# Queries loaded in half rows and turned on VectorE, remainder rows as one chunk, and a written order for all five engines

## The chip, the cores and the metric

The kernel runs on one core of a Trainium2 chip. The metric is the device time of one launch in microseconds (us), as the median of several runs. A profile is one execution of its own, recorded instruction by instruction. Engines are named as the profile names them: PE is TensorE's matmul, DVE is VectorE, ACT is ScalarE, POOL is GpSimd, SP issues the DMAs.

## The reference

Linear attention with two softmaxes, then a two-layer block with an odd activation:

```python
batch, n_heads, seq, head_dim = (8, 8, 576, 64)      # q, k, v
n_tokens, d_model, d_ff = (4608, 512, 2048)
q_s = softmax(q, over head_dim);  k_s = softmax(k, over seq)
kv = np.einsum('bhsd,bhse->bhde', k_s, v)
x = np.einsum('bhsd,bhde->bhse', q_s, kv)            # then (batch, seq) rows x (heads, 64) columns
h = x @ w_in
g = h - np.tanh(h)
out = g @ w_out
```

All is float32. The two large products are made of float32r matmuls on split operands (a rounded part and a remainder), three of the four cross products each.

## The kernel before

**Tiling.** The 4608 rows of x are nine chunks of 512 rows (`NCH = 9`); d_ff is sixteen tiles of 128. One *step* is one pair (chunk j, tile f). In it PE runs `ph`, twelve matmuls with 512 columns that make one tile of h in PSUM (line 568), and `po`, twelve matmuls that add the tile of g of two steps earlier (`LAG = 2`) into four PSUM tiles, one per 128 rows of output (line 651). There are 144 steps. Chunk 0 is done in two pieces, its first eight tiles ahead of chunk 1 and the rest behind it.

**The activation of a step.** From the PSUM tile `ph`, ACT makes `u` (square), `t` (tanh), `vv` (a square of u) and the mask `mk`; DVE makes `g` from u and ph (line 589), multiplies vv in (line 597), subtracts t from ph (line 594) and puts that result in where the mask is set (line 602, `cp`); ACT rounds it to `gh` (line 605); POOL makes the remainder `gl` (line 608). `gh` and `gl` are what `po` reads two steps later. These tiles have two buffers each, `ph` has two PSUM banks, `vv` and `mk` one buffer.

**Attention.** For each batch, k goes through a column maximum (`km` on DVE, `pm` transposes on PE, `mx`), a broadcast of it (`d` on POOL, `pb` on PE), a subtraction, an exponential and the products `pk` with v on PE; the normalised result is the tile `kvs`. A unit of q is 256 rows of all eight heads. Its softmax is a maximum per row and head (line 408, DVE), a subtraction (line 413, POOL), an exponential (ACT), a sum (line 421, DVE) and a product (line 447, POOL). Then every 128 rows are turned by four PE transposes into PSUM (`pt`, line 461), copied out by ACT (`qs`, line 473), and multiplied with `kvs` on PE (`px`, line 487); ACT and DVE split the result into `xh` and `xl`. Two batches have 1152 rows, nine tiles of 128, so that the last 64 rows of two batches make one tile (`rest`) and chunks and batches don't line up.

**The order.** `ORDER`, a list written by hand, sets all five engines for steps 0 to 18 with the whole weight preparation and the attention of batches 0 and 1. Behind it only PE and SP have a written order (line 784 and the loop below it), and the tool's own scheduler places the work of DVE, ACT and POOL. `prepare` (line 510) gives each attention part of a chunk a half step of the sixteen steps ahead of it.

Of the kernel before, what the change touches and what calls it, by code (L numbers as in the profile page):

```python
# [10 lines left out]
F32 = mybir.dt.float32  # L11
# [59 lines left out]
def attn_moe_kernel(  # L71
# [55 lines left out]
    kvs = [const.tile([P, NC, D], F32, name=f"kvs{i}") for i in range(3)]  # L127
# [145 lines left out]

    def kv_rows(b: int, st: dict):
# [13 lines left out]
        else:  # L288
            for n, m in enumerate((st["mh"], st["ml"])):
                d = ap.tile([P, NC, P], F32R, name=f"d{b}_{n}", tag="qs", bufs=3)  # L290
                nc.gpsimd.tensor_tensor(
                    d,
                    ident.unsqueeze(1).broadcast_to([P, NC, P]),
                    m.bitcast(F32).unsqueeze(2).broadcast_to([P, NC, P]),
                    op=ALU.mult,
                )
# [3 lines left out]
                    d.rearrange("p a m -> p (a m)"),  # L300
# [42 lines left out]
    def kv_norm(b: int, st: dict):  # L343
        nc.vector.tensor_tensor(
            kvs[b % 3],
            st["pk"][:, :, 1 : D + 1],
            st["rs"].broadcast_to([P, NC, D]),
            op=ALU.mult,
        )

    tiles = []
    for b in range(B):
        tiles += [((b, u), j) for u in range(NKP) for j in range(2)]
        if b % 2:
            tiles.append(((b, "rest"), 0))
    qs_of = {}

    def batches(i: int):
        (b, u), _ = tiles[i]
        return ((b - 1, 0, REST), (b, REST, P)) if u == "rest" else ((b, 0, P),)

    def rows_of(x: bass.AP, i: int):

        (b, u), j = tiles[i]
        if u == "rest":
            for bb, p0, p1 in batches(i):
                yield x[(bb + 1) * S - REST : (bb + 1) * S, :], p0, p1  # L370
        else:
            r0 = b * S + 2 * P * u
            yield x[r0 : r0 + 2 * P, :].rearrange("(p j) m -> p j m", j=2)[:, j, :], 0, P

    def q_load(unit):
        b, u = unit
        name = f"q{b}_{u}"
        if u == "rest":
            qt = ap.tile([P, H, 1, D], F32, name=name, tag="q", bufs=1)
            for half in range(2):  # L380
                src = q[b - 1 + half, :, S - REST :, :].rearrange("h s d -> s h d")
                nc.sync.dma_start(qt[half * REST : (half + 1) * REST, :, 0], src)
# [46 lines left out]
    def q_soft(unit):  # L429
        q_max(unit)  # L430
        q_sub(unit, nc.gpsimd)
        for part in (q_exp, q_sum, q_eps, q_inv):
            part(unit)
# [42 lines left out]
    px_of = {}  # L476

# [354 lines left out]
```

## Time and profile before

| | |
|---|---|
| time, median of 3 runs | 903.09 us (902.65 to 903.84) |
| span of the profiled execution | 901.7 us |
| PE busy | 875.9 us (97%) |
| DVE, ACT, POOL busy | 616.2, 554.2, 288.9 us |
| matmuls of L568 and L651 on the chain that ended last | 38% and 38% of the span |

The span runs from the first to the last instruction of the profiled execution; the median of the runs is 1.4 us above it. A group of matmuls is pipelined, so the time that it costs is the distance from its start to the start of the next group, not its duration. The number in square brackets behind a row of the timeline is idle time of that engine just ahead of it, with what ended it.

### The profile page before, as it was taken

The page shows a single profiled execution, that of the slowest core. Times are in us where ns is not written, and L with a number is a line of the kernel's source. Part 1 is how long each engine was busy: PE and PEld are TensorE (multiplying, and loading weights), DVE is VectorE, ACT ScalarE, POOL GpSimd, SP SyncE. Part 2 cuts the span into 40 slices and gives each one's busy share as a digit, 9 for nine tenths or more (in the row PEclk, how much of TensorE's full clock was granted, in tenths as well). Part 3 has the DMA queues.
Part 4 walks back from the last instruction along what each step waited for, and adds up shares of the span by engine and source line. Part 5 has one row for each costly group of instructions (what it writes and reads, how often), then busy time and mean ns, then how long its engine had stood idle before and what let it go on. Part 6 is the DMA issues. An engine that isn't in the chain of part 4 may idle for free.

```text
span 901.7 us, 13173 instructions
## 1 busy us (share of the span) xinstructions
PE 875.9 (97%) x5008; PEld 718.1 (80%) x5008; DVE 616.2 (68%) x906; ACT 554.2 (61%) x967; POOL 288.9 (32%) x246
## 2 busy tenths in 40 slices
PE   5899999999999999999999999999999999999997
PEld 5787778878778888888888888888888888888886
DVE  7999889957576767568656865865865566454444
ACT  4899986665455557555646565566656556556553
POOL 4641112433144324332333242332433233222221
PEclk7999999999999999999999999999999999999999
DMA  9993302030141402400141011401100020001001
GB/s 257 302 349 120 105 19 41 24 124 18 52 101 50 80 1 82 106 24 1 47 104 26 24 47 32 111 0 45 51 24 1 1 70 12 1 1 48 1 1 47
DMA packets 79775, 57.47 MB, mean 64 GB/s; under 512 B 14688, under 2 KB 72032, under 8 KB 79712
## 3 DMA queue, kind: packets, MB, share of 16 engines
q1 hardware_dynamic: 79712, 56.63, 22.2%
q8 instruction: 39, 0.64, 0.3%
q14 instruction: 24, 0.20, 0.1%
HBM read 46.14 MB, written 10.49 MB: 63 GB/s over the span
## 4 chain that ended last, share of the span: by engine, by line
PE 82%; DVE 8%; ACT 5%; DMA 2%; issue 1%; SPq 1%; POOL 0%; DVEq 0%; ACTq 0%; POOLq 0%
PE ph L568 38%; PE po L651 38%; PE pk L323 2%; PE px L487 2%; PE pt L461 2%; DMA k<-in_k_dram 1%; DVE g L589 1%; DVE t L594 1%; DVE g L597 1%; DMA raw_i<-in_moe_w_in_dram 1%; DVE g L602 1%; ACT mk L583 1%; DVE c_o L168 1%; DVE gl L608 1%; ACT gh L605 1%
## 5 line engine op out<-in xcount | busy, mean ns | idle before, releaser
L651 PE MATMUL po<-w_o,gh 128*128 128x512 f32 x1152 | 358.2, 392 | 0.3 <-DVE w_o L179 0.2
L568 PE MATMUL ph<-xh,w_i 128*128 128x512 f32 x1152 | 314.4, 395 | 4.7 <-DVE t L594 2.4
L608 POOL TENSOR_TENSOR gl<-g,gh 128x512 fp32r<-128x512 f32 x128 | 171.3, 1338 | 386.5 <-ACT gh L605 364.8
L568 PEld LDWEIGHTS ph<-xh,w_i 128*128 128x128 f32 x1152 | 214.1, 189 | 49.8 <-DVE t L594 2.8
L651 PEld LDWEIGHTS po<-w_o,gh 128*128 128x128 f32 x1152 | 214.5, 188 | 47.0 <-issue 1.5
L589 DVE SCALAR_TENSOR_TENSOR g<-u,ph 128x512 f32<-128x512 f32 x144 | 98.2, 682 | 204.6 <-ACT t L583 196.0
L651 PE MATMUL po<-w_o,gl 128*128 128x512 f32 x576 | 224.4, 390 | 0.0
L605 ACT CAST gh<-g 128x512 fp32r<-128x512 f32 x144 | 89.5, 621 | 180.6 <-DVE g L602 174.5
L568 PE MATMUL ph<-xl,w_i 128*128 128x512 f32 x576 | 155.9, 393 | 0.0
L597 DVE SCALAR_TENSOR_TENSOR g<-vv,g 128x512 f32<-128x512 f32 x144 | 117.8, 818 | 18.8 <-ACT vv L583 8.3
L583 ACT ACTIVATE u<-ph 128x512 f32<-128x512 f32 x144 | 85.9, 597 | 72.0 <-PE ph L568 71.8
L568 PEld LDWEIGHTS ph<-xl,w_i 128*128 128x128 f32 x576 | 109.1, 190 | 24.0 <-DVE xl L508 0.5
L651 PEld LDWEIGHTS po<-w_o,gl 128*128 128x128 f32 x576 | 108.1, 188 | 23.0
L602 DVE COPY_PREDICATED g<-mk,t 128x512 f32<-128x512 int32 x144 | 119.2, 828 | 3.4
L583 ACT ACTIVATE mk<-ph 128x512 int32<-128x512 f32 x144 | 86.4, 600 | 40.1 <-DVE g L589 38.2
L583 ACT ACTIVATE vv<-u,b_pa 128x512 f32<-128x512 f32 x144 | 104.6, 726 | 1.0 <-DVE g L597 1.0
L594 DVE TENSOR_TENSOR t<-ph,t 128x512 f32<-128x512 f32 x144 | 97.9, 680 | 6.3 <-ACT mk L583 5.6
L583 ACT ACTIVATE t<-ph 128x512 f32<-128x512 f32 x144 | 85.4, 593 | 3.0 <-DVE g L589 3.0
L413 POOL TENSOR_TENSOR q<-q,mq 128x1024 f32<-128x1024 f32 x14 | 28.0, 2002 | 50.5 <-DVE mq L408 48.7
L447 POOL TENSOR_TENSOR qn<-q,sq 128x512 f32<-128x512 f32 x30 | 34.6, 1153 | 27.2 <-PE pt L461 12.8
L408 DVE TENSOR_REDUCE mq<-q 128x16 f32<-128x1024 f32 x15 | 18.3, 1217 | 27.5 <-DMA q<-in_q_dram 27.5
L179 POOL TENSOR_TENSOR w_i<-c_i,w_i 128x512 fp32r<-128x512 f32 x12 | 18.2, 1527 | 39.1 <-ACT w_i L175 39.1
(94 smaller groups left out, 578.2 us busy)
## 6 DMA issues: line engine op xcount, KB each, us to landing
k<-in_k_dram SPq DMA_DIRECT2D x16, 512.0 KB, 6.3
raw_i<-in_moe_w_in_dram SPq DMA_DIRECT2D x16, 512.0 KB, 8.0
raw_o<-in_moe_w_out_dram SPq DMA_DIRECT2D x16, 512.0 KB, 8.9
q<-in_q_dram SPq DMA_DIRECT2D x15, 512.0 KB, 4.3
v<-in_v_dram SPq DMA_DIRECT2D x14, 512.0 KB, 5.8
out_dram<-o SPq DMA_DIRECT2D x28, 256.0 KB, 2.3
kr<-in_k_dram SPq DMA_DIRECT2D x8, 128.0 KB, 6.5
spare_v<-in_v_dram SPq DMA_DIRECT2D x2, 512.0 KB, 8.6
```

The lines of the kernel that those rows point to most:

```text
L408: nc.vector.tensor_reduce(mq, qf, axis=AX.X, op=ALU.max)
L413: eng.tensor_tensor(qf, qf, mq, op=ALU.subtract)
L447: eng.tensor_tensor(qn.rearrange("p a g d -> p g a d"), qt[:, :, j].rearrange("p (g a) d -> p g a d", g=2), sq[:, :, j : j + 1] .broadcast ...
L568: nc.tensor.matmul(ph, w[:, i, c], x[:, c, :], start=(n == 0), stop=(n == len(ops) - 1))
L583: nc.scalar.activation(new(tag, **of), st[src], fn, **kw)
L589: nc.vector.scalar_tensor_tensor(new("g"), st["u"], C2, st["ph"], op0=ALU.mult, op1=ALU.mult)
L594: nc.vector.tensor_tensor(st["t"], st["ph"], st["t"], op=ALU.subtract)
L597: nc.vector.scalar_tensor_tensor(st["g"], st["vv"], PB, st["g"], op0=ALU.add, op1=ALU.mult)
L602: nc.vector.copy_predicated(st["g"], st["mk"], st["t"])
L605: nc.scalar.copy(new("gh", F32R), st["g"])
L608: eng.tensor_tensor(new("gl", F32R), st["g"], st["gh"].bitcast(F32), op=ALU.subtract)
L651: nc.tensor.matmul(po[t], g[:, cols], wt["o", f][:, w], start=(begin and n == 0), stop=(end and n == 2),)
```

## The change

`ORDER` stays as it is. Behind it, from step 19 on:

- Units of batches 2 to 7 are loaded in another shape: a partition holds 32 of the 64 elements of a row, so a unit takes four DMAs of 32 partitions with runs of 128 bytes, where it took one with runs of 512. DVE reduces both halves and combines them over four small copies between groups of 32 partitions (`q_halves`). POOL's product is made in place. Two DVE block transposes (`q_flip`, line 511) take the place of the transposes on PE and of ACT's copies.
- Batches have 128 contiguous rows per tile. The last 64 rows of all eight batches are one chunk (j = 8), done between batches 6 and 7 (`ROUND`). For it each batch's kvs is written to DRAM (`kept`) and read back.
- All five engines have a written order. `PLACES` gives each attention part a place in a step (between `ph` and `po`, behind `po`, behind `cp` on DVE, behind `gl` on POOL and so on) and a step counted from the start of the chunk before; a chunk's sixteen steps are called its round below. `MOVED` has other places for three rounds.
- The mask is made from `u` and not from `ph` (`mu`). DVE takes two of the four output copies of a chunk. At step 32 the `po` of step 30 goes ahead of the `ph`.

```diff
+    tiles = [((b, u), j) for b in range(B) for u in range(NKP) for j in range(2)]
+    tiles += [((B, u), j) for u in range(B // 4) for j in range(2)]
...
+            for j, e in [(j, e) for j in range(2) for e in range(2)]:
+                p0, d = j * D + e * Q, slice(e * Q, (e + 1) * Q)
+                if b < B:
+                    src = quarters(q[b])[:, :, 2 * u * Q + j * Q :, :]
+                    runs = [(qt[p0 : p0 + Q], src[:, :, :Q, d])]
...
+                for dst, src in runs:
+                    to = "h l p d -> p h l d" if len(src.shape) == 4 else "h p d -> p h d"
+                    nc.sync.dma_start(dst, src.rearrange(to))
...
+    def q_halves(unit, name: str, op):
+
+        qf = qs_of[unit].rearrange("p h l d -> p (h l) d")
...
+        nc.vector.tensor_reduce(own, qf, axis=AX.X, op=op)
+        for n in range(P // Q):
+            at = n ^ 1
+            nc.vector.tensor_copy(other[at * Q : (at + 1) * Q], own[n * Q : (n + 1) * Q])
...
+    def q_flip(unit, g: int):
...
+        nc.vector.transpose(
+            qs.rearrange("p h t -> p (h t)"),
+            qs_of[unit][:, heads].rearrange("p h l d -> p (h l d)"),
+        )
...
+    def kv_other(b: int, st: dict):
+
+        for g in range(2):
+            rows, other = slice(g * D, (g + 1) * D), slice((1 - g) * D, (2 - g) * D)
+            nc.vector.tensor_tensor(
+                kvs[b % 2][rows, NC:],
...
+    PLACES = dict(
+        k=("sp", -6), v=("sp", -6), km0=("dve", -4), km1=("dve", -3), km2=("dve", -2),
+        km3=("dve", -1), pm=("end", 0), mx=("dve", 0), d=("pool", 0), pb=("mid", 2),
+        ks0=("dve", 3), ks1=("dve", 4), ke0=("act", 4), ke1=("act", 5), ker=("act", 6),
+        pk0=("mid", 5), v1=("pool", 5), pk1=("end", 7), den=("dve", 8), keep=("sp", 9),
+        back0=("sp", 8), back1=("sp", 10),
+        q0=("sp", -5), max0=("dve", -2), sub0=("pool", -2), exp0=("act", 0), sum0=("dve", 2),
+        n00=("pool", 2), n01=("pool", 3), f00=("dve", 4), f01=("dve", 5),
+        px0=("end", 9), xh0=("late", 9), xl0=("dve", 10),
+        q1=("sp", 5), max1=("dve", 7), sub1=("pool", 7), exp1=("act", 9), sum1=("dve", 9),
+        n10=("pool", 9), n11=("pool", 10), f10=("dve", 11), f11=("dve", 11),
+        px1=("end", 12), xh1=("late", 12), xl1=("dve", 13),
+    )
...
+            sum1=("dve", 13), den=("dve2", 13), keep=("sp", 14), n10=("pool", 13),
+            n11=("pool", 13), f10=("dve", 14), f11=("dve", 14),
+            px0=("end", 14), xh0=("post", 14), xl0=("post", 14),
+            px1=("end", 15), xh1=("post", 15), xl1=("post", 15),
...
+            mu=lambda: act("mk", "u", AF.Copy, scale=M_SCALE**2, dt=I32, bufs=1),
...
+        parts["ph"]()
+        more("mid")
+        for name in ("u", "t", "vv", "g", "tt", "mu", "gg"):
+            parts[name]()
+        more("sums")
+        more("end")
+        more("act")
+        parts["cp"]()
+        parts["gh"]()
+        more("late")
+        more("dve")
+        more("dve2")
+        parts["gl"](nc.vector if (j, f) == steps[-1] else nc.gpsimd)
+        more("pool")
+        more("post")
+        more("sp")
...
+            if n == 2 * NF:
+                add_sums()
```

The four lines behind `PLACES` are from the places of the first round (batch 2, steps 16 to 31) in `MOVED`; the last two are in the loop over the steps.

In the rows below a name is tile, chunk-free index and buffer number (`ph_12_4913` is tile f = 12), out<-in, and a form.

PE in the round of batch 4, around the second part of the products with v, before:

```order
L651 MATMUL po_0_3_4363<-w_o_877,gl_3_4408 128x512
L323 MATMUL pk_4460<-v_1_4477,k_1_4227 64x65 x16
L323 MATMUL pk_4460<-vr_4234,kr_4229 64x65 x8
L461 MATMUL pt_4566<-ident,qn_4564 128x128 x4
L568 MATMUL ph_6_4573<-xh_3835,w_i_779 128x512 x4
L568 MATMUL ph_6_4573<-xl_3836,w_i_779 128x512 x4
```

and after:

```order
L844 MATMUL po_0_3_4380<-w_o_958,gl_5_4550 128x512
L338 MATMUL pk_4503<-v_1_4552,k_1_3963 64x65 x16
L338 MATMUL pk_4503<-vr_3970,kr_3965 64x65 x8
L747 MATMUL ph_8_4678<-xh_3898,w_i_1312 128x512 x4
L747 MATMUL ph_8_4678<-xl_3899,w_i_1312 128x512 x4
```

The four transposes `pt` behind `pk` are gone, as are all 28 groups of them behind step 18; the groups of `ph`, `po`, `pk` and `px` stay.

DVE where the first unit of q of batch 6 gets its maximum, before:

```order
L408 TENSOR_REDUCE mq_0_5711<-q_0_5605 128x16
L589 SCALAR_TENSOR_TENSOR g_8_5568<-u_8_5564,ph_8_5551 128x512
L597 SCALAR_TENSOR_TENSOR g_8_5568<-vv_8_5570,g_8_5568 128x512
L594 TENSOR_TENSOR t_8_5566<-ph_8_5551,t_8_5566 128x512
L508 TENSOR_TENSOR xl_5600<-px_0_5581,xh_5599 128x2x256
L602 COPY_PREDICATED g_8_5568<-mk_8_5572,t_8_5566 128x512
L508 TENSOR_TENSOR xl_5600<-px_1_5582,xh_5599 128x2x256
L421 TENSOR_REDUCE sq_0_5715<-q_0_5605 128x16
L424 TENSOR_SCALAR sq_0_5715<-sq_0_5715 128x16
L427 RECIPROCAL sq_0_5715<-sq_0_5715 128x16
```

and after, at the end of a step and the start of the next:

```order
L781 COPY_PREDICATED g_14_5041<-mk_14_5044,t_14_5037 128x512
L263 TENSOR_TENSOR km_4973<-km_4973,k_1_4852 128x512
L485 TENSOR_REDUCE mq_6_0_5063<-q_0_4908 128x32
L488 COPY mq_6_0_5064<-mq_6_0_5063 32x32 x4
L500 TENSOR_TENSOR mq_6_0_5063<-mq_6_0_5063,mq_6_0_5064 128x32
L768 SCALAR_TENSOR_TENSOR g_15_5093<-u_15_5087,ph_15_5074 128x512
```

Before, the scheduler put attention parts between the parts of a step, also ahead of `cp`. Now they stand behind `cp` (line 781), and the maximum has four copies and a combination behind it. Two transposes stand in a row in step 11 of a round:

```order
L773 TENSOR_TENSOR t_11_4877<-ph_11_4862,t_11_4877 128x512
L776 SCALAR_TENSOR_TENSOR g_11_4881<-vv_11_4879,g_11_4881 128x512
L781 COPY_PREDICATED g_11_4881<-mk_11_4884,t_11_4877 128x512
L511 STREAM_TRANSPOSE qs_1_0_4902<-q_1_4555 128x512
L511 STREAM_TRANSPOSE qs_1_1_4904<-q_1_4555 128x512
L768 SCALAR_TENSOR_TENSOR g_12_4932<-u_12_4926,ph_12_4913 128x512
```

They hold DVE between the `cp` of that step and the first part of the next.

SP between the outputs of a chunk and the next loads, in the round of batch 4, before:

```order
L393 DMA q_1_4284<-in_q_dram 128x8x128
L680 DMA out_dram<-o_15_0_4289 128x512
L680 DMA out_dram<-o_15_1_4295 128x512
L680 DMA out_dram<-o_15_2_4301 128x512
L680 DMA out_dram<-o_15_3_4307 128x512
L235 DMA v_1_4477<-in_v_dram 128x8x128
L393 DMA q_0_4654<-in_q_dram 128x8x128
```

and after:

```order
L878 DMA out_dram<-o_15_0_4323 128x512
L878 DMA out_dram<-o_15_2_4326 128x512
L878 DMA out_dram<-o_15_1_4332 128x512
L878 DMA out_dram<-o_15_3_4335 128x512
L248 DMA v_1_4552<-in_v_dram 128x8x128
L431 DMA q_1_4555<-in_q_dram 32x32x32 x4
L379 DMA kept_111<-kvs_103 64x256 x2
L219 DMA k_0_4850<-in_k_dram 128x8x128
```

The load of the second unit of q was ahead of the outputs; now it is four DMAs and stands behind the load `v_1`, which waits for a POOL memset.

## Rows read from the trace of the kernel before

**Rows 1.** Page, part 1: busy time, share and instructions of each engine.

```profile
PE 875.9 (97%) x5008; PEld 718.1 (80%) x5008; DVE 616.2 (68%) x906; ACT 554.2 (61%) x967; POOL 288.9 (32%) x246
```

**Rows 2.** Busy time by stretch: stretch, length, each engine, clock, DMA share, GB/s.

```profile
600.00:700.00 100.00, 100.00 (x587) 81.94 (x586) 66.86 (x93) 58.99 (x102) 34.72 (x27) 1.00 0.09 27
```

**Rows 3.** Timeline of PE around transposes: start, duration, line, tiles, form, count.

```profile
740.03 1.07 PE L568 MATMUL ph<-xh,w_i 128*128 128x512 f32 x4
...
742.75 0.62 PE L651 MATMUL po<-w_o,gh 128*128 128x512 f32 x2
...
745.48 0.60 PE L461 MATMUL pt<-ident,qn 128*128 128x128 f32 x4
745.83 1.17 PE L568 MATMUL ph<-xh,w_i 128*128 128x512 f32 x4
...
748.66 0.62 PE L651 MATMUL po<-w_o,gh 128*128 128x512 f32 x2
```

**Rows 4.** Groups by line and form: count | busy, mean ns | idle before.

```profile
L461 PE MATMUL pt<-ident,qn 128*128 128x128 f32 x144 | 22.2, 278 | 0.0
```

**Rows 5.** Timeline of PE: the waits behind step 18, in square brackets.

```profile
186.95 1.15 PE L323 MATMUL pk<-v,k 128*64 128x65 f32 x32 [1.04 <-POOL gl L608]
...
232.77 1.22 PE L568 MATMUL ph<-xh,w_i 128*128 128x512 f32 x4 [1.59 <-ACT xh L506]
...
263.63 0.49 PE L297 MATMUL pb<-d,one_r 128*128 128x512 f32 x1 [0.15 <-POOL d L291]
264.77 0.50 PE L297 MATMUL pb<-d,one_r 128*128 128x512 f32 x1 [0.64 <-POOL d L291]
```

**Rows 6.** Timeline of all engines in a step without attention work.

```profile
428.44 0.61 PE L651 MATMUL po<-w_o,gh 128*128 128x512 f32 x2
...
429.83 0.69 DVE L589 SCALAR_TENSOR_TENSOR g<-u,ph 128x512 f32<-128x512 f32 x1 [2.57 <-ACT t L583]
...
431.16 1.07 PE L568 MATMUL ph<-xh,w_i 128*128 128x512 f32 x4
...
431.94 0.75 DVE L602 COPY_PREDICATED g<-mk,t 128x512 f32<-128x512 int32 x1
...
432.80 0.62 ACT L605 CAST gh<-g 128x512 fp32r<-128x512 f32 x1 [1.66 <-DVE g L602]
...
433.50 1.29 POOL L608 TENSOR_TENSOR gl<-g,gh 128x512 fp32r<-128x512 f32 x1 [4.15 <-ACT gh L605]
```

**Rows 7.** Groups by line and form, DVE: the parts nearest to new ones.

```profile
L508 DVE TENSOR_TENSOR xl<-px,xh 128x512 fp32r<-128x512 f32 x36 | 23.8, 679 | 1.2 <-ACT xh L506 1.2
...
L408 DVE TENSOR_REDUCE mq<-q 128x16 f32<-128x1024 f32 x15 | 18.3, 1217 | 27.5 <-DMA q<-in_q_dram 27.5
...
L250 DVE TENSOR_TENSOR km<-km,k 128x512 f32<-128x512 f32 x16 | 13.6, 852 | 2.2 <-DMA k<-in_k_dram 2.1
...
L157 DVE TENSOR_SCALAR raw_o<-raw_o 128x512 f32<-128x512 f32 x16 | 8.0, 509 | 0.0
...
L424 DVE TENSOR_SCALAR sq<-sq 128x16 f32<-128x16 f32 x16 | 4.6, 290 | 0.1
...
L344 DVE TENSOR_TENSOR kvs<-pk,rs 128x256 f32<-128x256 f32 x8 | 3.4, 422 | 0.2
```

**Rows 8.** DMA from 753 to 758 us: packets, MB, share; issues, KB each, landing.

```profile
q1 hardware_dynamic: 1056, 0.26, 14.5%
...
q_rest<-in_q_dram SPq DMA_DIRECT2D x2, 128.0 KB, 2.9
```

**Rows 9.** DMA from 266 to 273 us: the same columns.

```profile
q1 hardware_dynamic: 1040, 0.52, 26.3%
...
q<-in_q_dram SPq DMA_DIRECT2D x1, 512.0 KB, 4.0
```

**Rows 10.** Timeline of SP's queue: two loads of 128 KB, and the last outputs.

```profile
753.21 1.37 SPq L382 DMA_DIRECT2D q_rest<-in_q_dram  x2
...
895.63 3.32 SPq L680 DMA_DIRECT2D out_dram<-o  x5
```

More of the change, by code (lines that the diff above doesn't have):

```diff
@@ L288, in kv_rows @@
         else:
[L289 to L296, printed above, removed]
+            for n in range(2):
                 nc.tensor.matmul(
@@ L476, in attn_moe_kernel @@
     px_of = {}
+    ROUND = [*range(B - 1), B, B - 1]
     def x_mm(i: int):
@@ L483, in x_mm @@
             qs = qs_of.pop(i + n)
[L484 to L494 removed]
+            b = tiles[i + n][0][0]
@@ new lines, in x_mm, with kv_back @@
+            for a, g in [(a, g) for a in range(NC) for g in range(2)]:
+                rows, e0 = slice(g * D, (g + 1) * D), a % 2 * D
+                nc.tensor.matmul(
+                    px[g][e0 : e0 + D, a // 2, n * P : (n + 1) * P],
+                    kvs[b % 2][rows, a],
+                    qs[rows, a],
+                    start=True,
+                    stop=True,
+                    skip_group_check=True,
+                )
+    rest_kv = {}
+    def kv_back(u: int):
+        rest_kv[u] = t = ap.tile([P, 2, H, D], F32, name=f"rest_kv{u}", tag="k", bufs=NKP)
+        for j, g in [(j, g) for j in range(2) for g in range(2)]:
+            nc.sync.dma_start(t[j * D : (j + 1) * D, g], kept[4 * u + 2 * j + g])
@@ L518, in prepare, with at @@
+    def prepare(n: int, put):
+        j = ROUND[n]
+        places = PLACES | MOVED.get(n, {})
+        def at(name: str, call, *args):
+            place, step = places[name]
+            put(NF * (n - 1) + step, place, lambda: call(*args))
+        b = {B: B - 1, B - 1: None}.get(j, j)
+        if b is not None:
             st = {}
             for u in range(NKP + 1):
-                put(0, lambda u=u: k_load(b, st, u))
+                at("k", k_load, b, st, u)
             for u in (0, NKP):
-                for part in (v_ones, v_load):
-                    put(0, lambda u=u, part=part: part(b, st, u))
@@ L697, in attn_moe_kernel @@
     steps += [(0, f) for f in range(F0, NF)]
-    steps += [(j, f) for j in range(2, NCH) for f in range(NF)]
+    steps += [(j, f) for j in ROUND[2:] for f in range(NF)]
     pieces = []
@@ L752, in attn_moe_kernel, with put @@
     ENG = mybir.EngineType
-    ends = {}
+    calls = {}
+    def put(step: int, place: str, call):
+        calls.setdefault((step, place), []).append(call)
+    for n in range(2, NCH):
+        prepare(n, put)
+    for b in range(HALVED):
+        put(PLANNED + 1, "sp", lambda b=b: kv_keep(b))
     with tc.manual_schedule(engines={ENG.PE, ENG.DVE, ENG.Activation, ENG.Pool, ENG.SP}):
@@ L767, in attn_moe_kernel, with more, add_sums, put_out @@
             ops[name](*eng)
[L768 to L797 removed]
+        for n, (j, f) in enumerate(steps[PLANNED:], PLANNED):
+            def more(place: str, n=n):
+                for call in calls.pop((n, place), ()):
+                    call()
+            def add_sums(n=n):
+                o_step(*steps[n - LAG])
+            def put_out(t: int, call, n=n):
+                put(n, "dve" if t % 2 else "act", call)
+            more("first")
+            if n == 2 * NF:
+                add_sums()
+                put(n, "post", o_back)
+            else:
+                put(n, "sums", add_sums)
+            h_step(j, f, more)
+        assert not calls, list(calls)
+        def put_out(t: int, call):
+            call()
         for n in range(len(steps) - LAG, len(steps)):
```

314 lines of the change are left out of this document (193 added, 121 removed).

## Prediction

> **What bounds the kernel now.** I read the busy times first, then the same by stretch, then the timeline of PE. PE is busy for 97% of the span [rows 1], and in a stretch of the second half for all of 100 us, at a granted clock of 1.00, while DVE has work for two thirds of it and ACT and POOL for less [rows 2]. So behind the start the time is the sum of what stands on PE. A group of `ph` or of `po` takes 2.72 us (740.03 to 742.75) [rows 3]; a step is two of them, 5.44 us, and 144 steps are 783 us of the 901.7. The rest is the start, the attention work on PE, a few waits and the end. A change gains here by taking work off PE or by ending a wait of PE, and loses by making PE wait. Speeding up another engine gains nothing by itself.
>
> How far PE is from waiting is seen in a step without attention work [rows 6]. `ph` has ended when the next `po` starts, at 428.44. From there the chain goes through DVE's first part (429.83), `cp` (ends 4.25 us after `ph`), `gh`, and `gl`, which ends at 434.79, 6.35 us after. The `po` that reads it comes five groups later, 5 x 2.72 = 13.6 us after. So the chain has 7.2 us to spare in each step, and DVE has 2.57 us of idle time per step.
>
> **Transposes off PE.** The trace has 144 of them in groups of four [rows 4], 36 groups; the change leaves the 8 groups of batches 0 and 1 in `ORDER` and removes 28. A group holds PE for 0.35 us (745.48 to 745.83), and the twelve matmuls behind it take 2.83 us instead of 2.72, 0.11 more [rows 3]: 0.46 us in all. In six of the 28 the group stands right behind `pk`, where that loss of pace would be paid anyway; there I count 0.35. That is 22 x 0.46 + 6 x 0.35 = 12.2 us. It is at least 28 x 0.35 = 9.8 and at most 28 x 0.46 = 12.9. Nothing hides it, since PE has no idle time around these groups. ACT's 28 copies behind them go too, and are worth nothing.
>
> **Waits of PE behind step 18.** There are four: 1.04 us at the second `pk` of batch 2, 1.59 at the first `ph` of chunk 2, 0.15 and 0.64 at `pb` of batch 3 [rows 5], 3.4 us in all. The written places have cover for each: `pk1` comes two steps behind the load of v that it waits for, `po` of step 30 (2.72 us) stands between the last `px` and the `ph` of step 32, and `pb` stands two steps behind the `d` that it reads. I take all 3.4 off; the bounds are 0 and 3.4.
>
> **What DVE gets.** Per unit of q there are eight small copies, two combinations and two transposes more, per batch two parts for `kvs` on the other half of the partitions and two output copies. A 128x16 part took 0.29 us [rows 7], so I count 16 x 0.29 = 4.6 us per round for the copies, and 0.6 for the combinations (four, less two additions that fall away). The transposes are not in the trace. They touch 128x512 elements; the DVE parts of that size lie between 0.51 and 0.85 us [rows 7], and I bound them from 0.51 to 2.7, four times `xl`, since turning elements is nothing that a row shows. I take 0.68, that of `xl`, the same elements at the same width: 4 x 0.68 = 2.7 us. Two parts for `kvs` at 0.42 and two copies at 0.68 make 2.2. Together some 10 us in a round of about 92 us. DVE goes from 67% [rows 2] to 78%, and is still not the bound. In the fullest step, the one with a maximum and a `km`, 0.85 + 1.22 + 5 x 0.29 = 3.5 us stand in a gap of 2.57; the 0.95 us over go into the next step, which has one `km` of 0.9 and room. Lateness of DVE costs nothing until it uses up the 7.2 us. Cost: 0, and up to what rival C says.
>
> The Trainium skill, "VectorE: DVE Perf Modes", section "The three transpose paths", gives 311 ns for a 128x128 VectorE transpose in bf16 and only in blocks of 32x32, and its rules for kernel authors send a full 128x128 transpose to TensorE if PSUM is fine as its place, which speaks against this change. Four times 311 ns is an estimate of 1.2 us per transpose; by it the sum would be the same, as rival C's threshold shows. No row of this trace has such a transpose; the half-row layout makes the blocks enough.
>
> **The new mask.** `mk` is made from `u` in SBUF. It stands where `mk` stood, and lies beside PE's work; 0.
>
> **Loads of q.** The four DMAs move the bytes of one, in packets of 128 bytes: 4096, 256 per DMA engine. Packets of 256 bytes took 14.5% of 16 engines' 5 us for 1056 of them, 11 ns each [rows 8]; packets of 512 bytes took 26.3% of 16 engines' 7 us for 1040, 28 ns each, and their load landed in 4.0 us [rows 9], of which 65 packets are 1.8 us. Taking 11 and 28 ns as ends, 256 packets are 2.8 to 7.2 us, on 2.2 us that don't depend on them; the four issues, at 0.68 each [rows 10], put 2 us ahead. So 7 to 11.4 us from the first issue to the landing. The tightest place is the second unit: its issue in step 5 stands on SP behind `v_1`, which waits for a POOL memset behind `gl`, so it starts some 6.5 us after `ph` of step 5 has ended. Its maximum stands behind `cp` of step 7: two steps, one `pk` of 1.1 us [rows 5] and 4.25 us later, 16.2 us after. That leaves 9.7 us. DVE waits for 0 to 1.7 us there, and `g` of the next step is queued behind it; the 7.2 us cover that. Cost: 0.
>
> **The first round is denser.** Batch 2 has 13 steps for what a later batch has 20 for. In step 13 DVE has a sum with four copies, a combination and a reciprocal (1.22 + 6 x 0.29 = 3.0 us) and the parts of `kvs` (3 x 0.29 + 3 x 0.42 = 2.1) [rows 7], from 4.25 us after `ph` to 9.35; `px0` on PE wants `kvs` three groups, 8.16 us, after the same point. PE waits 1.2 us there, and I take that for the round, with 0 and 4 as ends.
>
> **The end.** The last output tile was two pieces and is one. An issue took 0.66 us [rows 10], the second one falls away: 0.4 less, between 0 and 0.66.
>
> **The sum.** 901.7 - 12.2 - 3.4 + 1.2 - 0.4 = 886.9 for the span, and 1.4 around it: 888.3, say 888 us, 1.7% under 903.1.
>
> **Rivals.** *B, a written order that waits a little in each round.* DVE, ACT and POOL each stand in one order with parts that wait for one another, where before a scheduler filled gaps. DVE has 78% of its time taken and a step overfull in each round. One us of PE in each of seven rounds gives 895. For it: DVE's parts lengthen beside POOL's, so my sums are low. Against it: 7.2 us to spare, and no place where my count reaches PE in a later round.
>
> *C, transposes at four times the price.* Two stand in a row in step 11, from 4.25 us after `ph`, and `px1` follows three groups, 8.16 us, after it. So they cost nothing up to (8.16 - 4.25) / 2 = 1.95 us each. At 2.7 PE waits 1.5 us in six rounds, 9 us, and some 4 in the first: 888 + 13 = 901, which is no change by this measurement (it can tell about 0.2%, 1.8 us).
>
> *D, the short runs land late: slower.* The place is the maximum of the second unit. Room of 9.7 us and 7.2 of the chain make 16.9 us from first issue to landing; beyond that each us is a us of PE, in seven rounds. At 19.3 us the gain is gone and 1.8 us more, at 25 us it is 888 + 7 x 8.1 = 945. Against it: the rows give 7 to 11.4. By the Trainium skill, "DMA: Bandwidth & Descriptors", Specifications, a transfer under 512 bytes is read, modified and written back. Were each packet two accesses at 28 ns, the load would take 2 + 2.2 + 14.4 = 18.6 us, near the point where it decides; the packets of 256 bytes in this trace took less than those of 512, so the rows don't bear it out.
>
> *E, better than the sum,* by waits that I don't see in the rows: under 885.
>
> **How the numbers follow.** Forecast 0.62 (885 to 891), B 0.20 (891 to 898), C 0.07, D 0.07, E 0.04. The predicted time is 888. The range from 885 to 898 takes in the forecast with the ends of its unknown terms and B, 0.82. Faster by over 0.2% (under 901.3) are the forecast, B, E and nearly half of C: 0.89. Within 0.2%: the rest of C, 0.04. Slower: D, 0.07.
>
> **What would show it.** Right: no `pt` on PE behind step 18, PE at 100% in all stretches from 200 us on with groups of 2.72 us, no waits of more than 1 us on PE behind step 31, and DVE near 78%. C shows as transposes over 1.95 us and idle time of PE ahead of `px` named after them. D shows as DVE's reduction waiting for q, and a landing over 16.9 us. B shows as idle time of PE at the same step of each round. The sum is wrong if `px` or `pk` take longer on PE than before, since I left their groups alone.

## The result, and the profile after

The changed kernel takes 888.88 us in the median of 4 runs (888.16 to 889.78), the kernel before 903.1. The ratio is 0.9843, with a 95% interval from 0.9825 to 0.986. The forecast was 888.0, with a range from 885 to 898. The profiled execution has a span of 887.7 us, against 901.7 before. One of five executions of the changed kernel in a later run took 1232 us at a granted clock of 0.65, and is left out below.

Page of the changed kernel, part 1 (busy us, share of the span, instructions), beside [rows 1]:

```profile
PE 863.2 (97%) x4896; PEld 707.5 (80%) x4896; DVE 653.7 (74%) x1078; ACT 528.3 (60%) x923; POOL 280.6 (32%) x244
```

Busy time by stretch in the changed kernel, the stretch and columns of [rows 2]:

```profile
600.00:700.00 100.00, 100.00 (x626) 82.18 (x626) 72.74 (x124) 56.19 (x99) 32.21 (x27) 1.00 0.22 39
```

PE has 112 matmuls and 12.7 us of work less, and is still busy for the whole of that stretch. DVE has 37.5 us more work, ACT 25.9 less.

The table of waits of PE behind step 18 (line, waited for, us in total, times, longest), beside the four of [rows 5], which are all gone:

```profile
PE po L844 <- DVE back L865: 2.1, 1, 2.1
PE px L605 <- DVE kvs L370: 0.5, 1, 0.5
PE px L605 <- DVE kvs L359: 0.2, 1, 0.2
```

The two at `px` are the denser first round, 0.70 us in all. The one at `po` was in no term of the sum. DVE's timeline around it (start, duration, line, form, count; in brackets the idle time before and what ended it):

```profile
238.19 0.76 DVE L781 COPY_PREDICATED g<-mk,t 128x512 f32<-128x512 int32 x1
238.84 0.68 DVE L263 TENSOR_TENSOR km<-km,k 128x512 f32<-128x512 f32 x1
239.56 0.68 DVE L266 TENSOR_TENSOR km<-km,kr 64x512 f32<-64x512 f32 x1
240.16 1.20 DVE L485 TENSOR_REDUCE mq<-q 128x32 f32<-128x1024 f32 x1
241.40 0.73 DVE L488 COPY mq<-mq 32x32 f32<-32x32 f32 x4
242.17 0.19 DVE L500 TENSOR_TENSOR mq<-mq,mq 128x32 f32<-128x32 f32 x1
242.28 0.68 DVE L768 SCALAR_TENSOR_TENSOR g<-u,ph 128x512 f32<-128x512 f32 x1
...
244.82 1.28 DVE L865 TENSOR_TENSOR back<-po,back 128x512 f32<-128x512 f32 x2
```

PE's timeline at the same place:

```profile
245.65 0.70 PE L844 MATMUL po<-w_o,gh 128*128 128x512 f32 x2 [2.08 <-DVE back L865]
```

Here chunk 0 ends, the one that is done in two pieces: DVE adds the sums of its first piece (`back<-po`), and the next chunk's first `po` wants the banks that these four additions empty. Ahead of those additions two `km` parts and a whole maximum of the queries stand on DVE, and no idle time is left between `cp` (238.19) and `g` of the next step (242.28).

The new parts of DVE, groups by line and form (count | busy us, mean ns | idle before), beside [rows 7]:

```profile
L488 DVE COPY sq<-sq 32x32 f32<-32x32 f32 x56 | 21.9, 391 | 1.0
L511 DVE STREAM_TRANSPOSE qs<-q 128x512 f32<-128x512 f32 x28 | 18.7, 691 | 0.0
L488 DVE COPY mq<-mq 32x32 f32<-32x32 f32 x56 | 17.0, 304 | 1.0
...
L370 DVE TENSOR_TENSOR kvs<-pk,rs 64x256 f32<-64x256 f32 x12 | 5.1, 422 | 0.3
```

And the last outputs on SP's queue, beside the second row of [rows 10]:

```profile
882.34 2.48 SPq L878 DMA_DIRECT2D out_dram<-o  x4
```

### The profile page after: what moved, and what is told of

It reads as the page before. It is cut to its first block, busy times and chain, and to the rows that moved or that the text cites. A ratio compares the mean times of both kernels' runs of the same rounds, so it can differ in the third digit from the quotient of the medians.

```text
span 887.7 us, 13369 instructions
## 1 busy us (share of the span) xinstructions
PE 863.2 (97%) x4896; PEld 707.5 (80%) x4896; DVE 653.7 (74%) x1078; ACT 528.3 (60%) x923; POOL 280.6 (32%) x244
## 4 chain that ended last, share of the span: by engine, by line
PE 83%; DVE 8%; ACT 5%; DMA 2%; issue 1%; SPq 1%; DVEq 0%; ACTq 0%
PE ph L747 39%; PE po L844 39%; PE pk L338 2%; PE px L605 2%; DVE g L768 1%; DMA raw_i<-in_moe_w_in_dram 1%; DMA k<-in_k_dram 1%; ACT mk L762 1%; DVE t L773 1%; DVE g L776 1%; DVE g L781 1%; DVE c_o L181 1%; DVE gl L787 1%; ACT raw_o L177 1%; DVE k L324 1%
## 5 line engine op out<-in xcount | busy, mean ns | idle before, releaser
L787 POOL TENSOR_TENSOR gl<-g,gh 128x512 fp32r<-128x512 f32 x128 | 167.9, 1312 | 478.1 <-ACT gh L784 456.1
L747 PE MATMUL ph<-xh,w_i 128*128 128x512 f32 x1152 | 313.2, 394 | 3.1 <-DVE t L773 2.4
L747 PEld LDWEIGHTS ph<-xh,w_i 128*128 128x128 f32 x1152 | 214.8, 189 | 50.5 <-DVE t L773 2.8
L747 PE MATMUL ph<-xl,w_i 128*128 128x512 f32 x576 | 155.8, 392 | 0.0
L747 PEld LDWEIGHTS ph<-xl,w_i 128*128 128x128 f32 x576 | 109.2, 190 | 23.7 <-DVE xl L637 0.3
L781 DVE COPY_PREDICATED g<-mk,t 128x512 f32<-128x512 int32 x144 | 110.1, 765 | 13.3 <-DVE g L776 0.5
L776 DVE SCALAR_TENSOR_TENSOR g<-vv,g 128x512 f32<-128x512 f32 x144 | 106.9, 742 | 0.3
L762 ACT ACTIVATE mk<-u 128x512 int32<-128x512 f32 x125 | 79.0, 632 | 0.0
L496 POOL TENSOR_TENSOR q<-q,sq 128x512 f32<-128x512 f32 x28 | 29.4, 1053 | 18.4 <-DVE sq L476 17.1
L637 DVE TENSOR_TENSOR xl<-px,xh 128x512 fp32r<-128x512 f32 x36 | 23.1, 685 | 0.0
```

The lines of the kernel that those rows point to most:

```text
L496: nc.gpsimd.tensor_tensor(part, part, of, op=op)
L637: nc.vector.tensor_tensor(xl, px, xh.bitcast(F32), op=ALU.subtract)
L747: nc.tensor.matmul(ph, w[:, i, c], x[:, c, :], start=(n == 0), stop=(n == len(ops) - 1))
L762: nc.scalar.activation(new(tag, **of), st[src], fn, **kw)
L776: nc.vector.scalar_tensor_tensor(st["g"], st["vv"], PB, st["g"], op0=ALU.add, op1=ALU.mult)
L781: nc.vector.copy_predicated(st["g"], st["mk"], st["t"])
```

## The experiments

**One ruler for all of them.** The start of the program is the same in both kernels, and the times of one kernel differ there from execution to execution (the section on the hardware shows by how much). So beside the median time, the runs are compared by a stretch that leaves the start out: from the first matmul of `ph` in step 19 to the start of DVE's last copy of an output tile. From it two things are taken off: PE's waits in it, and what PE lost to a lower granted clock, summed over pieces of 5 us as (1 - granted clock) x length. What is left is PE's own work. The ratio is to the kernel before on the same chip, as the runs were made on several (it took 902.9 to 903.6 us on them). The four right columns are of one profiled execution each.

| run | median us | ratio to before (95%) | stretch | waits of PE | lost to the clock | left |
|---|---|---|---|---|---|---|
| before | 903.1 | | 754.43 | 3.42 | 0.00 | 751.01 |
| changed | 888.88 | 0.9843 (0.9825 to 0.986) | 741.21 | 2.78 | 0.00 | 738.43 |
| changed, again | 889.43 | 0.9847 (0.9832 to 0.9862) | 741.17 | 2.75 | 0.00 | 738.42 |
| changed, PE's groups put back | 902.54 | 0.9997 (0.9987 to 1.0007) | 755.60 | 2.61 | 1.70 | 751.29 |
| before, groups left out | 892.35 | 0.9881 (0.9862 to 0.9899) | 745.25 | 4.93 | 1.70 | 738.62 |
| maximum later | 886.98 | 0.982 (0.9804 to 0.9836) | 739.81 | 1.35 | 0.00 | 738.46 |
| two waits removed | 888.07 | 0.983 (0.9811 to 0.9848) | 739.84 | 1.65 | 0.00 | 738.19 |
| and `pb` at the end | 887.1 | 0.9817 (0.9802 to 0.9832) | 738.84 | 1.09 | 0.00 | 737.75 |
| DVE's transposes twice | 890.05 | 0.9842 (0.9825 to 0.9859) | 742.79 | 2.78 | 1.70 | 738.31 |
| DVE's transposes four times | 900.28 | 0.9966 (0.9953 to 0.9979) | 753.21 | 11.26 | 1.70 | 740.25 |
| one quarter of the load twice | 890.15 | 0.9858 (0.9843 to 0.9873) | 741.34 | 2.90 | 0.00 | 738.44 |
| the load twice | 926.74 | 1.0256 (1.0239 to 1.0272) | 777.29 | 25.85 | 15.50 | 735.94 |
| the load three times | 986.47 | 1.0921 (1.0894 to 1.0949) | 840.47 | 85.11 | 46.05 | 709.31 |

In the last two rows the low clock also covers time in which PE was waiting, so that time is taken off twice, and "left" comes out too small there.

### PE's groups put back into the changed kernel

```diff
         w = wt["i", f].rearrange("p t (c f) -> p t c f", c=NC)
+        if steps.index((j, f)) in range(20, 132, 4):
+            for a in range(NC):
+                nc.tensor.transpose(ph[:, a * P : (a + 1) * P], ident, ident)
```

> The changed kernel with the old load of TensorE put back and nothing else: ahead of ph in 28 steps of the second chunk on (every fourth) four transposes of the 128x128 identity go into the bank that ph then overwrites. They compute nothing that is used; VectorE still turns the queries and the written order stays. Theory, by the sum of the prediction (a group of four costs PE 0.35 to 0.46 us on top of the matmuls beside it, and PE has no slack): 28 x 0.46 = 12.9, so 888.9 + 12.9 = 901.8 us, bounds 898.7 to 901.8. Rival, that the gain came from the new order of the engines and that PE has room for the groups: 888 to 890 us.

Measured: 902.54 us, 0.7 over the upper bound, and 0.9997 (0.9987 to 1.0007) of the kernel before: the gain is gone. PE's timeline in this run, where L747 is the added group and `ph` stands three lines lower than in the changed kernel:

```profile
612.13 1.07 PE L750 MATMUL ph<-xh,w_i 128*128 128x512 f32 x4
...
617.57 0.60 PE L747 MATMUL ph<-ident 128*128 128x128 f32 x4
617.93 1.17 PE L750 MATMUL ph<-xh,w_i 128*128 128x512 f32 x4
...
623.48 0.60 PE L272 MATMUL pm<-ident,km 128*128 128x128 f32 x4
```

A step without a group takes 617.57 - 612.13 = 5.44 us, the one with it 623.48 - 617.57 = 5.91, so 0.47 for a group. By the ruler PE's own work grew by 751.29 - 738.43 = 12.86 us, 0.46 for each of the 28. Of the 14.39 us by which the stretch grew, the other 1.5 are the lower clock (1.70) less 0.17 of waits.

### The groups left out of the kernel before

```diff
             put(turn, lambda i=i: q_norm(i, nc.gpsimd))
-            put(turn, lambda i=i: q_turn(i))
-            put(turn, lambda i=i: q_keep(i))
+            put(turn, lambda i=i: q_as_is(i))
```

> The kernel before with the turning of the 28 query tiles left out (TensorE's transposes and ScalarE's copies of them), so the products take the queries unturned, which is other arithmetic of the same size; the order, the loads and the small last tiles stay as in before. Theory: 903.1 - 12.2 = 890.9 us, and the four waits of PE behind step 18 (3.4 us together) stay, so it ends about 2 us above the changed kernel. Rival, that the gain came from the written order: 902 to 903 us, with new waits of PE where the groups stood.

Measured: 892.35 us, 10.6 less than before on the same chip (902.92), where 12.2 was expected. The trace tells what works against the 12.2; it is of the slowest of the four executions (894.49), with a stretch 9.18 us shorter than before. The table of PE's waits behind step 18 in this run:

```profile
PE ph L570 <- ACT xh L509: 1.7, 1, 1.7
PE pb L297 <- POOL d L291: 1.5, 2, 0.9
PE po L653 <- POOL gl L610: 1.0, 2, 0.5
PE pk L323 <- POOL qn L447: 0.7, 1, 0.7
```

Those are 4.93 us for 3.42, 1.51 more: `ph` and `pb` wait longer, `pk` less, and the two waits at `po` are new. Another 1.70 us went to the clock in this execution. PE's own work fell by 751.01 - 738.62 = 12.39 us, near the 12.2 of the sum, and it ends 0.2 us from that of the changed kernel. So the written order and the other edits changed PE's own work by nothing that shows. What the new order shows instead is fewer waits: 2.78 us, where the order of before, relieved of the same groups, has 4.93.

### The maximum one step later

```diff
-            q0=("sp", -2), max0=("dve", 0), sub0=("pool", 0), exp0=("act", 2),
+            q0=("sp", -2), max0=("dve2", 1), sub0=("pool", 1), exp0=("act", 2),
```

> The changed kernel with one edit of its table, in the third round: VectorE's maximum of the first unit (with its four 32x32 copies) and GpSimd's subtraction move from step 0 to the end of step 1, behind the additions that free the po banks. Theory, that PE's 2.08 us wait at po of step 34 is VectorE's lateness (4.3 us of attention work in a gap of 2.6 us): the wait falls to 0 to 1 us and the time to 886.9 to 887.8 us (the changed kernel: 888.9). Rival, that the additions wait for the sums to come back by DMA: the wait stays within 0.3 us of 2.08 and the time at 888.9. Second rival, that the work is as late one step on: the wait goes to another place behind it, and the time stays.

Measured: 886.98 us. The wait at `po` of step 34 is gone, and behind it a smaller one appears in PE's timeline of this run:

```profile
254.82 0.50 PE L312 MATMUL pb<-d,one_r 128*128 128x512 f32 x1 [0.67 <-POOL d L289]
```

The stretch is shorter by 1.40 us, 2.08 less 0.67. So the additions were late because DVE was, and not because the sums to be added came late. Of the second rival a third came true. The subtraction of the queries now stands ahead of `d` on GpSimd, but does not hold it up: GpSimd is idle for 2.26 us between the two, and `d` ends 12.8 us behind the start of `pm` (241.96 to 254.77), against 12.9 in the changed kernel (242.97 to 255.91). It is `pb` that comes sooner, 11.8 us behind `pm` for 14.1.

### Both waits taken away

```diff
-            sum1=("dve", 13), den=("dve2", 13), keep=("sp", 14), n10=("pool", 13),
+            sum1=("dve2", 13), den=("dve", 13), keep=("sp", 14), n10=("pool", 13),
...
-                put(n, "dve" if t % 2 else "act", call)
+                put(n, "dve" if t % 2 and n != 2 * NF + 1 else "act", call)
```

> As the run with the later maximum, and two more edits of places: in step 33 all four additions that free the po banks stand ahead of copy_predicated (two stood on either side of ScalarE's slot), and in the second round the denominators and normalisation of the keys stand one slot ahead of the second unit's sum. Theory: both waits of PE that are left behind step 18 (2.08 at po, 0.70 at px of the first round) go, 888.9 - 2.8 = 886.1 us, range 885.5 to 887.5. Rival, that the additions so early hold up copy_predicated of step 33 and with it gl and po of step 33 or 34: PE waits 1 to 3 us there, 887 to 890 us.

Measured: 888.07 us (886.35 to 889.73), above the expected range and no gain over the run before it. Both waits are gone, but `pb` now waits twice, 1.65 us together, where the run before it had waits of 1.35 in all; PE's timeline of this run:

```profile
253.13 0.50 PE L312 MATMUL pb<-d,one_r 128*128 128x512 f32 x1 [0.71 <-POOL d L289]
254.57 0.50 PE L312 MATMUL pb<-d,one_r 128*128 128x512 f32 x1 [0.94 <-POOL d L289]
```

In the changed kernel `pb` did not wait, because the 2.08 us ahead of it had given `d` the time. The rival had the time right (887 to 890 us), but named another place (`gl`), where nothing waits. The next run moves `pb`:

```diff
-            pm=("mid", 2), mx=("dve", 2), d=("pool", 2), pb=("mid", 4), ks0=("dve", 4),
+            pm=("mid", 2), mx=("dve", 2), d=("pool", 2), pb=("end", 4), ks0=("dve", 4),
```

> The run with both waits taken away (later maximum, the four additions ahead of copy_predicated, the denominators ahead of the sum) and one edit more: in the third round pb moves on PE from the middle of its step to the end. There pb waited twice for GpSimd's d (0.71 + 0.94 = 1.65 us), since d ends about 2 us behind the place in the middle, and the end of the step is some 2.7 us later. Theory: no wait of PE is left behind step 18, 2.78 us less from the start of ph of step 18 to the last copy of the output than the changed kernel's 741.21, so 738.4, and a time of 886.1 us; if the early part starts as in the run before, 885. Rival, that pb so late holds up the subtraction of the keys and with it pk: a wait of 0.5 to 2 us there, 886.5 to 888.

Measured: 887.1 us (885.33 to 887.38), 0.9817 (0.9802 to 0.9832) of before. Against the run before, the stretch is 1.0 us shorter where 1.4 was expected (0.56 us of waits and 0.44 of PE's own work). The rival came true: the keys are exponentiated later, and `pk` waits, as PE's timeline of this run shows.

```profile
264.35 1.15 PE L338 MATMUL pk<-v,k 128*64 128x65 f32 x32 [1.09 <-ACT k L327]
```

The stretch is 2.37 us shorter than in the changed kernel (738.84 for 741.21), which is the best of all runs. On the same chip the changed kernel took 889.43 in the median; the intervals of the two ratios touch at 0.9832, so the times by themselves barely part the two, and the trace does.

### DVE's transposes done twice and four times

```diff
-        nc.vector.transpose(
+        for _ in range(4):
+            nc.vector.transpose(
```

> The changed kernel with each of VectorE's 28 transposes of a half tile done twice (the second writes the same again): 1.38 us for 0.69 each. Theory, by the threshold of the prediction's third rival (two transposes stand in step 11 ahead of the second unit's products; each may take up to 1.95 us before PE waits): no more than 1 us over 888.9, no new waits of PE above 0.5 us. Rival, that VectorE at 74 per cent has no room left (its share would go to about 76 per cent plus 28 x 0.69 = 19 us of work on the steps with a transpose): 19 us on the path at most, some 895 to 908 us.

> The changed kernel with each of VectorE's 28 transposes done four times: 2.76 us each, as the dear end that the prediction's third rival took from the costliest row. Theory: past the threshold of 1.95 us; two in step 11 are 2 x (2.76 - 1.95) = 1.6 us late at the second unit's px in each of seven rounds, 11 to 13 us together, 900 to 902 us. Rival, that the products wait elsewhere or the lateness is caught up: 889 to 893 us. Rival on the other side, that the lateness adds to the next steps (gl late for po): above 905 us.

Measured: twice, 890.05 us, 1.15 over 888.9 where at most 1 was said, but with the ratio of the changed kernel (0.9842 for 0.9843), with the same three waits as in the changed kernel (2.78 us) and nothing else that is longer on PE; the 1.58 us by which its stretch is longer are the 1.70 us lost to the clock. Four times, 900.28 us, inside the expected 900 to 902. There PE waits where it was said to, at the second unit's `px`; rows of the table of PE's waits in the run with four:

```profile
PE px L606 <- DVE qs L512: 5.8, 6, 1.1
PE px L606 <- DVE xl L638: 2.3, 2, 2.1
```

The total agrees better than its parts. A wait is 0.94 us in five rounds and 1.14 in one, where 1.6 was said: `px` starts on the first half's transposes, and its other 16 matmuls alone wait for the second half's. The new 2.3 us stand in the first round; and 1.7 us of clock and 1.8 of own work (the interrupted groups of `px`) make up the rest. What the two runs show is that the threshold lies between 1.4 and 2.8 us for each transpose.

### The second unit's queries loaded later

```diff
-                for dst, src in runs:
+                for dst, src in runs * (2 if u and b < B else 1):
```

> The changed kernel with the second unit's query load of each chunk but the last issued twice into the same tile, the second set behind the first on SP's queue and, as it writes the same rows, behind its landing. The load so lands about 4 us later, 12 to 14 us from the first issue instead of 7 to 11. Theory, by the prediction's fourth rival (room of 9.7 us up to VectorE's maximum and 7.2 us of spare time behind it: the point is 16.9 us): VectorE waits 2 to 4 us for the queries in a round, PE does not, and the time stays within 1 us of 888.9. Rival, that VectorE has no spare time in a step: the wait of VectorE is passed on, seven rounds of 2 to 4 us, 903 to 917 us.

> The same load issued three times, each set behind the landing of the one before: landed 17 to 20 us from the first issue. Theory: at or past the point of 16.9 us, so PE waits 0 to 3 us in each of seven rounds: 889 to 910 us, most likely 895 to 903, and the waits stand at po or ph behind a late gl. Rival, that the spare time of 7.2 us is larger than the chain shows: no change, 888 to 890 us. Rival, that it is smaller: VectorE's wait beyond 9.7 us passed on whole, 7 x 8 = 56 us, 940 us or above.

Measured: 926.74 and 986.47 us. The first is far over the theory and its rival; the second is far over the theory and lies where its last rival had it (940 or above), though DVE's waits for queries are not passed on whole: 49.4 us of them with two loads and 110.4 with three, against 23.1 and 82.3 us more of PE's waits. Part of the miss is the experiment's: issued twice, the queries landed later than the 12 to 14 us that I expected. SP's queue in one round of the run with two:

```profile
581.79 15.56 SPq L431 DMA_DIRECT2D q<-in_q_dram  x8
```

DVE's timeline in that round:

```profile
599.58 1.22 DVE L485 TENSOR_REDUCE mq<-q 128x32 f32<-128x1024 f32 x1 [8.35 <-DMA q<-in_q_dram]
...
605.65 0.42 DVE L359 TENSOR_TENSOR kvs<-pk,rs 128x256 f32<-128x256 f32 x1
```

PE's timeline in that round:

```profile
606.22 0.40 PE L605 MATMUL px<-qs,kvs 64*64 64x128 f32 x2 [3.44 <-DVE kvs L359]
607.11 1.56 PE L605 MATMUL px<-qs,kvs 64*64 64x128 f32 x30 [0.49 <-DVE kvs L370]
608.60 2.08 PE L747 MATMUL ph<-xh,w_i 128*128 128x512 f32 x4
```

The maximum, which waits for the landing, starts 599.58 - 581.79 = 17.8 us after the first issue. The point was to be 16.9, so a wait of 0.9 us was due, and it is 3.4 + 0.5. The reason is in the place: PE does not wait at a `po` for `gl`, but at the first unit's `px` for `kvs`, which stands one step behind the maximum on DVE. DVE's timeline in the same round of the changed kernel shows the slack up to there:

```profile
560.77 1.21 DVE L485 TENSOR_REDUCE mq<-q 128x32 f32<-128x1024 f32 x1
...
565.51 0.69 DVE L768 SCALAR_TENSOR_TENSOR g<-u,ph 128x512 f32<-128x512 f32 x1 [1.71 <-ACT t L762]
...
569.20 0.86 DVE L370 TENSOR_TENSOR kvs<-pk,rs 64x256 f32<-64x256 f32 x2
```

And the `px` that reads it, on PE's timeline of the changed kernel:

```profile
572.37 1.10 PE L605 MATMUL px<-qs,kvs 64*64 64x128 f32 x32
```

DVE has 1.71 us of idle time behind the maximum, and `kvs` ends 2.31 us ahead of `px`: 4.0 us, not 7.2. From the first issue (551.44) to the maximum are 9.3. So the point is 13.3 us. By it the run with two loads should wait 17.8 - 13.3 = 4.5 us (3.9 measured in this round), and the run with three, whose load lands 28.1 us after its first issue (648.30 against 620.20), 14.8 (14.0 measured: 13.73 and 0.24). Counted back from these waits the point is 13.9 and 14.1 us.

The load was repeated in six rounds (not seven, as was expected), and five of them have `kvs`. The sixth, of the last chunk, has none, and there the run with two loads, landing at 16.0 us, makes PE wait nowhere. In the run with three, DVE's timeline and PE's in that round, where the first issue is at 821.32:

```profile
848.47 1.22 DVE L485 TENSOR_REDUCE mq<-q 128x32 f32<-128x1024 f32 x1 [16.89 <-DMA q<-in_q_dram]
...
851.93 2.07 PE L747 MATMUL ph<-xh,w_i 128*128 128x512 f32 x4 [9.69 <-DVE t L773]
```

Here the point is 848.47 - 821.32 - 9.69 = 17.5 us, and the reader is the `ph` that wants the bank which DVE's `t` reads. So one engine, late by the same part, has a different slack in each of the two kinds of round.

That point was tested once more with a smaller delay:

```diff
-                for dst, src in runs:
+                for dst, src in runs * (2 if u and b < B and j + e == 0 else 1):
```

> The changed kernel with the first of the four loads of the second unit's queries issued twice (the second waits for the first to land), in each chunk but the last. The run that issued all four twice landed 17.8 us from the first issue, VectorE waited 8.2 us in a round, and PE 22.4 us in all. Here the landing should be at 11 to 13 us. Theory, as mended by that run (9.3 us of room up to the maximum and 1.7 + 2.3 = 4.0 us of slack behind it, up to px that needs the normalised keys: the point is 13.3 us): VectorE waits 2 to 4 us in a round and PE at most 0.3 us, 888 to 890 us. Theory as in the prediction (point 16.9 us): the same here. Rival, that PE loses whatever VectorE waits, and half as much again by a lower granted clock: 7 x 3 x 1.5 = 31 us, some 905 to 925 us.

Measured: 890.15 us, just over the expected 890, against 889.43 for the changed kernel on the same chip, and its stretch is 0.13 us longer. The load lands 10.9 us after its first issue (551.55), DVE waits, PE waits no more than in the changed kernel (2.90 us for 2.78); DVE's timeline of this run:

```profile
562.46 1.22 DVE L485 TENSOR_REDUCE mq<-q 128x32 f32<-128x1024 f32 x1 [1.46 <-DMA q<-in_q_dram]
```

It does not part 13.3 from 16.9 by itself, as it lies under both; the runs with two and three loads do that. It shows that a wait of DVE under the point costs nothing.

The waits are not the whole price of the late loads. The run with two has 23.1 us of waits more than the changed kernel, and is 36.1 us longer in the stretch. Busy time by stretch in the same round of the run with two (stretch, length, PE busy, ..., granted clock third from the end):

```profile
600.00:606.00 6.00, 2.78 (x13) 1.97 (x11) 5.68 (x14) 0.73 (x2) 1.95 (x2) 1.00 0.00 0
606.00:608.00 2.00, 1.29 (x27) 1.11 (x30) 1.92 (x5) 2.00 (x5) 1.24 (x1) 0.90 0.16 41
608.00:610.00 2.00, 2.00 (x16) 1.43 (x9) 1.90 (x4) 1.13 (x3) 0.00 (x0) 0.50 0.58 145
610.00:612.00 2.00, 2.00 (x8) 1.58 (x7) 1.95 (x3) 1.42 (x3) 1.29 (x1) 0.75 1.15 318
612.00:614.00 2.00, 2.00 (x11) 1.65 (x10) 1.02 (x6) 1.24 (x3) 0.79 (x1) 1.00 0.70 160
```

Behind the wait the granted clock falls from 1.00 to 0.50, that is from 2.4 to 1.2 GHz, and four matmuls of `ph` take 2.08 us instead of 1.07. PE loses 0.2 + 1.0 + 0.5 = 1.7 us behind a wait of 3.4.

## Why the prediction was right, and where it was not

The time came out as said, and the largest term is shown by two runs that do it in opposite directions. The small terms were off in ways that nearly cancel, which is luck: 886.9 for the span, + 2.08 (not foreseen) - 0.50 - 0.25 - 0.38 - 0.09 (step 19 starts that much earlier) = 887.8, where 887.7 was measured. Two of the signs of being right did not come: a wait of over 1 us stands on PE behind step 31 (the 2.08 us), and DVE is not near 78%.

- **Transposes off PE, 12.2 us (9.8 to 12.9): right.** 12.58 by the ruler between the two kernels (0.38 more), 12.86 when put back, 12.39 when taken out of before. The way of counting held: 0.35 for the group and 0.11 for the pace that the matmuls behind it lose.
- **Four waits of PE, 3.4 us: right.** None of [rows 5] is left.
- **The first round, 1.2 us: right place, 0.70 us (0.50 less).** The wait is at `px0` and for `kvs`, as said.
- **The end, 0.4 us: 0.65 (0.25 more).** The copy starts at 897.08 and 883.77, with 4.61 and 3.96 us from there to the end of the span (901.69 and 887.73).
- **"Lateness of DVE costs nothing until it uses up the 7.2 us": this step failed.** The 7.2 us were to be those of the chain from `ph` through `gl` to `po`, in a step without attention work [rows 6], and they are one group too many. Between the end of a `ph` and the `po` that reads its `gl` stand four groups, not five (`po`, `ph`, `po`, `ph`; in the order of the kernel before, `gl_3` is read ahead of `ph_6`): 10.9 us, less 6.35, is 4.5. And DVE also feeds PE by other ways. Where chunk 0 ends, the additions free the banks of the next chunk's first `po`, and a step that was overfull just there cost 2.08 us. The count of the fullest step (3.5 us in 2.57) fits this step in size (3.4 us, 238.95 to 242.36), but the prediction had one `km` and room in the step behind it, and here the four additions stand there: the run with the later maximum removed the wait. At the second unit's load the first user is `kvs`, with 4.0 us. The forecast didn't suffer because the load landed early.
- **"DVE near 78%": 74% for the span, 72.7% in the stretch of [rows 2].** The added work was counted about rightly: 38.9 us for copies (4.6 a round said, 5.6 here), 18.7 for transposes, 5.1 for `kvs`, 9.0 for output copies. But two parts that every step has got shorter, which I had not foreseen. Groups of DVE before (count | busy us, mean ns | idle before):

```profile
L602 DVE COPY_PREDICATED g<-mk,t 128x512 f32<-128x512 int32 x144 | 119.2, 828 | 3.4
L597 DVE SCALAR_TENSOR_TENSOR g<-vv,g 128x512 f32<-128x512 f32 x144 | 117.8, 818 | 18.8 <-ACT vv L583 8.3 <-DVE g L589 0.5 <-DVE sq L427 0.3
```

The same two groups in the changed kernel:

```profile
L781 DVE COPY_PREDICATED g<-mk,t 128x512 f32<-128x512 int32 x144 | 110.1, 765 | 13.3 <-DVE g L776 0.5
L776 DVE SCALAR_TENSOR_TENSOR g<-vv,g 128x512 f32<-128x512 f32 x144 | 106.9, 742 | 0.3
```

That is 20.0 us of DVE's time, 0.14 us in each of the 18 steps of 100 us, about half of what is missing from the 78%; the rest was not followed up. Which edit did it was not tried, and since DVE is not the bound it moved nothing that shows.
- **Copies at 0.29 us and transposes at 0.68: 0.30 to 0.39, and 0.69.** The row that I took for the transposes, the same elements at the same width, was the right one. Rival C needed over 1.95 us each. Its mechanism is real (the run with four times), only its price wasn't paid.
- **Loads of q, 7 to 11.4 us: 7.3 here, the low end.** The first of the four DMAs starts at 551.44, the last lands at 558.76, and DVE's maximum at 560.77 waits for nothing. In the other rounds of batches 2 to 7 it was 5.8 to 8.6 us. A packet of 128 bytes took 13 to 20 ns (last section), within the 11 to 28. Rival D's mechanism is real too, but its numbers were off: where `kvs` is made, the point is 13.3 to 14.1 us and not 16.9, and a us beyond it costs more than a us of PE, because the clock falls behind the wait. At a landing of 17.8 us the kernel is already 23 us slower than before; by the prediction it would still have been faster (888 + 7 x 0.9 = 894).
- **Rival B, a wait in each round: not seen.** The two waits in the first round and the one where chunk 0 ends are all.

## What to carry to other kernels

Slack is not a number of an engine but of a pair: for each result of the engine that gets more work, find who reads it and how long before that reader comes, and take the shortest, above all where a chunk or a batch ends. When a wait is removed, look at what stood idle behind it: its neighbours were fed by the same wait (here `pb`, then `pk`), and the gain is what the next one leaves. And where the engine that bounds the time is made to wait, count the slower clock behind the wait too.

## What the runs showed of the hardware that was not expected

**The clock behind short waits.** PE's granted clock could fall to half behind a wait of only 2 us, and did so in some executions and not in others. The same wait at the start of step 18, on PE's timeline of the profiled execution of the changed kernel:

```profile
135.61 2.08 PE L747 MATMUL ph<-xh,w_i 128*128 128x512 f32 x4 [2.39 <-DVE t L773]
```

And on that of the changed kernel run again:

```profile
135.54 1.19 PE L747 MATMUL ph<-xh,w_i 128*128 128x512 f32 x4 [2.35 <-DVE t L773]
```

The first execution comes to step 19 at 142.56 us, the second at 141.12, and from there on they take 741.21 and 741.17. That is 1.44 us, beside 1.6 between the lowest and the highest time of this kernel (888.16 to 889.78); the other executions have no trace, so what made them differ is not shown. Wherever the clock fell behind one short wait it cost 1.70 us: behind the 2.06 us at `po` with PE's groups put back, the 1.75 us at `ph` in the kernel before without them, the 2.08 us at `po` with the transposes twice, and the 2.14 us at `px` with the transposes four times. So in these runs a wait of 2 us cost 2 us or nearly 4. Behind the longer waits of the late loads (3.4 to 17 us) the clock fell each time.

**A small packet takes less time than a large one, but more for its bytes.** Between 587 and 600 us of the run with two loads nothing but queries is moved, in packets of 128 bytes (packets, MB, share of 16 engines):

```profile
q1 hardware_dynamic: 7280, 0.92, 45.3%
```

That is 0.453 x 16 x 13 us / 7280 = 12.9 ns for a packet, against 11 for the 256 bytes of [rows 8]: a packet of 128 bytes took about as long as one of 256, and less than half of one of 512 bytes [rows 9], which has four times the bytes. With more loads at once it took longer: in the changed kernel, from 556 to 557 us, 1081 packets of queries filled 137.3% of 16 engines' time, 20 ns each. The rule of the Trainium skill ("DMA: Bandwidth & Descriptors", Specifications) that a transfer under 512 bytes is read, modified and written back shows in no such row; the 56 ns of two accesses, as rival D had them, are not reached.

**DVE turned 128x512 elements at the pace of a plain part of that size.** It took 691 ns in blocks of 32x32 (and 708 in the run with four in a row), with `xl` at 685 ns in the same trace. The estimate of 1.2 us, worked out from the Trainium skill's 311 ns for 128x128 in bf16 ("VectorE: DVE Perf Modes", "The three transpose paths"), was too high by 0.5 us.
